# Backward attention: all score gradients transposed by DMA, two units to a transfer

## The chip, the cores and the metric

The kernel runs on one core of a Trainium2 chip. The metric is device time in microseconds (us) of one execution; the number quoted is the median of the runs. A core has TensorE (matrix products, results in PSUM), VectorE, ScalarE and GpSimd (elementwise work), SyncE (SP), which here only starts DMAs, and 16 DMA engines that all queues share. Each engine works through its own instructions in order and waits on semaphores for the others.

## The reference

The reference is one transformer block with conditioned layer norms, and the gradients of its output with respect to nine of its inputs. The sequence has 2048 tokens of 512 features, attention has 32 heads of 16.

```
h = layernorm(x) * (1 + ca) + sa
q, k, v = heads of (h @ wqkv)
p = softmax(q k^T / 4);  x = x + ga * ((p v) @ wo)
h = layernorm(x) * (1 + cb) + sb
x = x + gb * (relu(h @ w1 + b1)^2 @ w2 + b2)
output: x, and the gradients of sum(x * grad_out) for x, wqkv, wo, w1, b1, w2, b2, c, w_mod
```

The change lies in the backward pass of the attention. For each head it needs, with E = p and dP = dO v^T, the matrix dS = E * (dP - rowsum), 2048 x 2048, and from it dK = dS^T q, dV = E^T dO and dQ = dS k.

## The kernel before

Four stages follow each other: projections, forward attention with the feed-forward part and its gradients chunk by chunk, the backward attention loop (1122 to 2409 us in the profile), and a last stage for the remaining gradients.

The backward loop works in units (`units`). A unit is one group of four heads (`hg`), one chunk of 512 keys (`kc`) and one tile of 128 queries (`qc`, `qi`): a piece of 128 queries x 4 heads x 512 keys. There are 8 x 4 x 4 x 4 = 512 units. Four units with the same `hg`, `kc` and `qc` make a block, so there are 128 blocks; unit number `u` belongs to block `u // 4`.

For one unit the work is:

- `score`: four products of 32 x 128 with 32 x 512 into PSUM banks A, B or C (line 1595), one a head. The operands are padded by rows that bring the softmax's maximum and denominator along.
- `expo`: ScalarE takes the exponential of each into the tile `E_u` (line 1601).
- `dp_pair` (a `D` in the order): for two heads at a time two products into `psD_u` (line 1613), and VectorE multiplies them with `E_u` into the tile `dS_u`, 128 x 2048 of bf16, 512 KB (line 1615). Two `D` make a unit's dS.
- `transpose_unit`: after a unit's second `D`, SP starts a transposing DMA from `dS_u` into the unit's quarter of the block's tile `dsT` (line 1628). dQ needs dS with keys on the partitions.
- `k_quad` and `v_quad` (each a `q`): four products each that add the unit's dK and dV to a PSUM bank (lines 1650 and 1659). They read `dS_u` and `E_u` as they are.
- `dq_quad` (in a `d`) and `dq_out` (`Q`): for a whole block, 16 products of `dsT` with the keys (line 1677), and the sum's way out of PSUM by ScalarE (lines 1687 and 1690) and GpSimd (1695).

In every second block (`on_pe`), the fourth unit isn't transposed by DMA. TensorE turns it instead: `pe_turn` (`t1`, `t2`) does eight 128 x 128 transposes into PSUM (line 1640), and ScalarE copies them into `dsT` (`T1`, `T2`, line 1756). So 448 units go over SP's queue and 64 over TensorE.

The order of the work is written out by hand for TensorE, ScalarE, VectorE, SP and GpSimd. Two lists of tokens, `order_n` and `order_t`, each describe one block; block `b` takes `order_t` if block `b - 1` has a TensorE turn. `order_t` has the tokens of the turn and four `f`, which let TensorE do a small product without effect (`keep_warm`, line 1633). In a list, the `s` and `e` belong to block `b`; the `D` run one pair behind them, so a block's last `D` is the first `D` in the next block; the `d1`, `d2` and `Q` belong to block `b - 2`.

How far the stages may run ahead of each other is set by the number of tiles: six of `dS_u`, four of `E_u`, three of `dsT`. A tile is written again when all that read it have finished, so a `dS_u` tile is held until its transfer has landed and its k quad is done. Loads for the next head group are started from ScalarE's queue (`plan_head`), 64 KB each; in the last head group SP itself starts five loads of 512 KB (line 1547).

Of the kernel before, what the change touches and what calls it, by code (L numbers as in the profile page):

```python
# [14 lines left out]
AF = mybir.ActivationFunctionType  # L15
ALU = mybir.AluOpType
AX = mybir.AxisListType
BF = dt.bfloat16
F32 = dt.float32

P = 128
D = 512
# [12 lines left out]
def kernel(  # L35
# [17 lines left out]
    PE = nc.tensor  # L53
    DVE = nc.vector
    ACT = nc.scalar
    POOL = nc.gpsimd
    SP = nc.sync
# [4 lines left out]
    identb = persist.tile([P, P], BF, name="identb")  # L62
# [84 lines left out]
    with ExitStack() as ph:  # L147
# [4 lines left out]
        ework = att.enter_context(tc.tile_pool(name="phCe", bufs=4))  # L152
# [1048 lines left out]
        def head_fill(i):  # L1201
            for key in ("k", "v", "q", "do"):
                POOL.memset(hsets[i][key][:], 1.0 if key in ("k", "v") else 0.0)
# [345 lines left out]
    with ExitStack() as ph:  # L1549
        tpool = ph.enter_context(tc.tile_pool(name="phIt", bufs=3))  # L1550
        ework = ph.enter_context(tc.tile_pool(name="phIe", bufs=4))
        wk = ph.enter_context(tc.tile_pool(name="phIw", bufs=2))
        psd = ph.enter_context(tc.tile_pool(name="psId", bufs=2, space=bass.MemoryType.PSUM))
        psx = ph.enter_context(tc.tile_pool(name="psIx", bufs=1, space=bass.MemoryType.PSUM))
        units = [(hg, kc, qc, qi) for hg in range(HG) for kc in range(QC) for qc in range(QC) for qi in range(4)]
        NU = len(units)
        hst, bst, sst, dqt, cur = {}, {}, {}, {}, {}

        def load_head(hg):
            st = dict(hsets[hg % 2])  # L1560
            st["qz"] = qz[hg % 2]
            st["acc"] = stg.tile([P, n], F32, name="dQacc", tag="dQacc", bufs=1)
            st["dq"] = stg.tile([P, n], BF, name="dQst", tag="dQst", bufs=1)
            st["vk"] = stg.tile([P, n], BF, name="vkb", tag="vkb")
            hst[hg] = st
# [22 lines left out]
        def score(u, hq, bank):  # L1588
            hg, kc, qc, qi = units[u]
            st = hst[hg]  # L1590
            qt = qc * 4 + qi
            r = 32 * hq
            psS = psx.tile([P, 512], F32, name=f"psS_{bank}", tag=banks[bank])
            sst[u, hq] = psS
            PE.matmul(psS[:], st["q"][r:r + 32, qt * P:(qt + 1) * P], st["k"][r:r + 32, kc * 512:kc * 512 + 512],  # L1595
                      start=True, stop=True, tile_position=(r, 0))

        def expo(u, hq):
            if hq == 0:
                bst[u] = [ework.tile([P, 4, 512], BF, name="E_u", tag="E_u"), None]  # L1600
            ACT.activation(bst[u][0][:, hq, :], sst.pop((u, hq))[:], AF.Exp, scale=SCALE)  # L1601

        def dp_pair(u, pair):
            hg, kc, qc, qi = units[u]
            st = hst[hg]
            qt = qc * 4 + qi
            if pair == 0:
                bst[u][1] = ework.tile([P, 4, 512], BF, name="dS_u", tag="dS_u", bufs=6)
            E_u, dS_u = bst[u]
            psD = psd.tile([P, 2, 512], F32, name="psD_u", tag="pd")  # L1610
            for hi in range(2):
                r = 32 * (2 * pair + hi)
                PE.matmul(psD[:, hi, :], st["do"][r:r + 32, qt * P:(qt + 1) * P], st["v"][r:r + 32, kc * 512:kc * 512 + 512],  # L1613
                          start=True, stop=True, tile_position=(r, 0))
            DVE.tensor_tensor(dS_u[:, 2 * pair:2 * pair + 2, :], psD[:], E_u[:, 2 * pair:2 * pair + 2, :], ALU.mult)  # L1615
            if qi == 3 and on_pe(u // 4):
                held["dS"] = dS_u

        def on_pe(b):
            return b % 2 == 1  # L1620

        def transpose_unit(u):
            hg, kc, qc, qi = units[u]
            if qi == 0:
                dqt[u // 4] = tpool.tile([P, 4, 16, P], BF, name="dsT", tag="dsT")
            if qi == 3 and on_pe(u // 4):
                return
            SP.dma_start(out=dqt[u // 4][:, qi], in_=bst[u][1].rearrange("p h k -> p (h k)"), transpose=True)

        held = {}  # L1630

        def keep_warm():
            PE.matmul(cur["vk"][0:DH, :], KS_tok[:, 0, D:QPAD], dOs_tok[:, 0, :], start=False, stop=False,
                      tile_position=(0, 0), skip_group_check=True)

        def pe_turn(b, half):
            pt = psx.tile([P, 8, P], BF, name="ptT", tag="px")
            for i in range(8):
                kt = i % 4
                PE.transpose(pt[:, i, :], held["dS"][:, 2 * half + i // 4, kt * P:(kt + 1) * P], identb[:])  # L1640
            dst = dqt[b][:, 3, 8 * half:8 * half + 8, :]
            held[half] = (dst, pt)

        def k_quad(u):
            hg, kc, qc, qi = units[u]
# [34 lines left out]
        def dq_out(b):  # L1680
# [17 lines left out]
                    r = hg % 2 * 64 + hq * DH  # L1698
                    at(cur["j"] + 6 + hq, load, dQc[hg // 2, r:r + DH, :], st["dq"][32 * hq:32 * hq + DH, :])

        order_t = (
            "s0 s1 q s2 e0 e1 D s3 D e2 s4 e3 t1 e4 q T1 D "
            "s5 s6 e5 f f t2 e6 s7 T2 e7 D s8 e8 D f f s9 e9 q q s10 "
            "s11 e10 D d1 d2 e11 Q q s12 D e12 s13 e13 q s14 D e14 "
            "s15 q q e15 ").split(), "ABCABBABACABABCA"
        order_n = (
            "s0 D s1 q e0 q s2 e1 e2 D s3 s4 q s5 e3 D e4 "
            "e5 s6 q s7 D s8 e6 e7 d1 e8 s9 D d2 e9 q Q s10 "
            "s11 e10 D q s12 e11 e12 s13 e13 D q s14 s15 e14 e15 D q ").split(), "CBACBACBABABCABC"
# [6 lines left out]
        with tc.manual_schedule(engines={PE.engine, ACT.engine, DVE.engine, SP.engine, POOL.engine}):  # L1716
            head_fill(1)
            POOL.memset(qz[1][:], 0.0)
            nD, nq = -1, -4
            idle = psx.tile([P, 512], F32, name="idle", tag="accVK")  # L1720
            for b in range(NU // 4 + 3):
                toks, bank = order_t if on_pe(b - 1) else order_n
                for tok in toks:
                    c, i = tok[0], int(tok[1:] or 0)
                    if c == "s" and b < NU // 4:
                        if i == 0 and units[4 * b][1:] == (0, 2, 0) and units[4 * b][0] + 1 < HG:
                            load_head(units[4 * b][0] + 1)
                        score(4 * b + i // 4, i % 4, bank[i])
                    elif c == "e" and b < NU // 4:
                        expo(4 * b + i // 4, i % 4)  # L1730
                        if b < 2 and i % 2 == 1:
                            if nq > 0:
                                keep_warm()
                            elif nq < 0:
                                PE.matmul(idle[:], ones_bf[:], identb.unsqueeze(1).to_broadcast([P, 4, P]), start=True, stop=True)
                    elif c == "D":
                        if 0 <= nD < 2 * NU:
                            dp_pair(nD // 2, nD % 2)
                            if nD % 2 == 1:
                                transpose_unit(nD // 2)  # L1740
                        nD += 1
                        cur["j"] = nD
                        for j in sorted(j for j in todo if j <= nD):
                            for f, args in todo.pop(j):
                                f(*args)
                    elif c == "q":
                        if 0 <= nq < 2 * NU:
                            (v_quad if nq % 2 else k_quad)(nq // 2)
                        nq += 1
                    elif c == "f" and 0 < nq < 2 * NU:  # L1750
                        keep_warm()
                    elif c == "t" and 0 <= b - 1 < NU // 4:
                        pe_turn(b - 1, i - 1)
                    elif c == "T" and 0 <= b - 1 < NU // 4:
                        dst, pt = held.pop(i - 1)
                        ACT.activation(dst, pt[:], AF.Identity)  # L1756
                    elif c == "d" and 0 <= b - 2 < NU // 4:
                        for kt in (2 * i - 2, 2 * i - 1):
                            dq_quad(b - 2, kt)
                    elif c == "Q" and 0 <= b - 2 < NU // 4:  # L1760
                        dq_out(b - 2)
            assert not todo
        dq_last = hst[HG - 1]["dq"]

    with ExitStack() as ph:
# [15 lines left out]
        order = (("vk", 6), ("vk", 0), ("vk", 1), ("vk", 2), ("vk", 3), ("dq", 0), ("vk", 7), ("dq", 1), ("vk", 4), ("dq", 2), ("vk", 5), ("dq", 3))  # L1781
# [140 lines left out]
        with tc.manual_schedule(engines={PE.engine, ACT.engine, DVE.engine}):  # L1922
            for k, (key, i) in enumerate(order):
                for g in range(2):
                    if (2 * k + g) % 2 == 0:
                        pt = pst.tile([P, 8, P], BF, name="ptq", tag="ptq")
                    else:
                        pt = psd.tile([P, 8, P], BF, name="ptd", tag="pdh1")
                    for ti in range(8):
                        t = 8 * g + ti  # L1930
                        PE.transpose(pt[:, ti, :], xs[key, i][:, t * P:(t + 1) * P], identb[:])
                    if key == "dq":
                        dst = dq_tok[:, 8 * g:8 * g + 8, i * P:(i + 1) * P]
                    else:
                        dst = dvk_tok[:, 8 * g:8 * g + 8, i, :]
# [32 lines left out]
            for b in range(3):  # L1968
                for ic in range(DC):
                    dwqkv(b, ic)  # L1970
                    i = b * DC + ic
# [75 lines left out]
```

## Time and profile before

| | |
|---|---|
| median of 3 runs | 2542.18 us (2538.7 to 2542.64) |
| profiled execution, first to last instruction | 2533.7 us |
| its whole time | not given |
| TensorE products | 2353.2 us (93%), 19005 instructions |
| ScalarE | 2305.1 us (91%), 3577 instructions |
| VectorE | 1808.8 us (71%), 2317 instructions |
| backward loop: dS multiplications on VectorE | 1024 x 1216 ns |
| backward loop: exponentials on ScalarE | 2048 of 650 to 661 ns |
| backward loop: dS transfers on SP | 448, median 2670 ns on SP's queue |
| backward loop: copies after TensorE's turns on ScalarE | 128 x 1128 ns |

The page of a profile gives busy times of the engines, the span in 40 slices, the DMA queues, the chain of work that ended last and the costliest groups. Queries of the trace give single stretches of it: the instructions of one line or tile, the time order of one engine, and sums by stretch. A time on SP's queue is the time that SP itself was occupied with starting a DMA; the transfer lands later. Neighbouring exponentials overlap in ScalarE's pipeline, so their durations add up to more than the time they take.

### The profile page before, as it was taken

How to read it: one execution, taken by the hardware profiler on the slowest of the kernel's cores; microseconds unless marked ns; L12 is line 12 of the kernel's file. 1: busy time of each engine (PE TensorE's matmuls, PEld its weight loads, DVE VectorE, ACT ScalarE, POOL GpSimd, SP SyncE). 2: the span in 40 equal slices, each digit the busy share in tenths (PEclk: the TensorE clock that was granted, in tenths of full speed). 3: DMA queues.
4: the chain of work that ended last, by engine and by line, in shares of the span. 5: the costliest groups of instructions: out<-in, count | busy, mean ns of one | idle time of the engine just before them, and what ended most of it. 6: DMA issues, size and time to landing. Idle time of an engine off the chain costs nothing.

```text
span 2533.7 us, 50560 instructions
## 1 busy us (share of the span) xinstructions
PE 2353.2 (93%) x19005; PEld 777.5 (31%) x19005; DVE 1808.8 (71%) x2317; ACT 2305.1 (91%) x3577; POOL 348.5 (14%) x370
## 2 busy tenths in 40 slices
PE   7898889989988998999999999999999999999999
PEld 3232223223322323533232223232232322332343
DVE  5555153454444455579899999899998998998872
ACT  7999999999999999549999999999999998998952
POOL 2000001211323141110101101011010110100100
PEclk9999999999999999999899999999999999999999
DMA  6477454366649765979999999999999999999972
GB/s 204 126 191 190 140 130 128 90 164 144 94 101 193 129 144 119 276 199 194 189 201 199 198 197 203 197 195 201 206 202 195 202 195 199 202 203 207 200 241 73
DMA packets 1227131, 447.21 MB, mean 177 GB/s; under 512 B 1103096, under 2 KB 1197752, under 8 KB 1226631
## 3 DMA queue, kind: packets, MB, share of 16 engines
q1 hardware_dynamic: 1198966, 409.14, 81.9%
q0 software_dynamic: 10944, 16.78, 4.6%
q10 hardware_dynamic: 16976, 18.07, 2.6%
q8 instruction: 149, 2.44, 0.4%
q14 instruction: 96, 0.78, 0.1%
HBM read 96.75 MB, written 73.95 MB: 67 GB/s over the span
## 4 chain that ended last, share of the span: by engine, by line
PE 41%; ACT 37%; DVE 7%; issue 7%; DMA 5%; SPq 2%; ACTq 0%; POOL 0%; DVEq 0%; POOLq 0%
ACT E_u L1601 23%; ACT ET L562 11%; PE dqacc L1677 5%; PE psST L560 4%; PE psS_A L1595 3%; PE pm L233 3%; DMA dsT<-dS_u 2%; PE accVK L1650 2%; PE oacc L576 2%; PE psS_B L1595 2%; ACT dsT L1756 2%; PE pdh L1871 2%; PE psS_C L1595 2%; SPq L178 2%; PE pm L412 2%
## 5 line engine op out<-in xcount | busy, mean ns | idle before, releaser
L1615 DVE TENSOR_TENSOR dS_u<-psD_u,E_u 128x1024 bf16<-128x1024 f32 x1024 | 1186.1, 1216 | 93.0 <-PE psD_u L1613 27.2
L562 ACT ACTIVATE ET<-psST 128x1024 bf16<-128x1024 f32 x1024 | 942.7, 1240 | 23.4 <-PE psST L560 22.7
L1601 ACT ACTIVATE E_u<-psS_A 128x512 bf16<-128x512 f32 x768 | 507.8, 661 | 14.1 <-DMA out_dram<-xlast 7.2
L1601 ACT ACTIVATE E_u<-psS_B 128x512 bf16<-128x512 f32 x768 | 501.2, 653 | 8.9 <-PE psD_u L1613 2.2
L1613 PE MATMUL psD_u<-iv,ido 32*128 32x512 bf16 x2048 | 412.0, 390 | 5.4 <-DVE dS_u L1615 5.2
L560 PE MATMUL psST<-qt_sb,kt_sb 32*128 32x512 bf16 x2048 | 315.7, 387 | 50.4 <-ACT ET L562 45.5
L1601 ACT ACTIVATE E_u<-psS_C 128x512 bf16<-128x512 f32 x512 | 332.8, 650 | 13.4 <-DMA dsT<-dS_u 9.9
L1595 PE MATMUL psS_A<-ik,iq 32*128 32x512 bf16 x768 | 296.2, 386 | 11.2 <-ACT E_u L1601 1.1
L1595 PE MATMUL psS_B<-ik,iq 32*128 32x512 bf16 x768 | 297.1, 387 | 9.4 <-ACT E_u L1601 1.9
L1595 PEld LDWEIGHTS <-iq 32*128 32x128 bf16 x2048 | 130.0, 91 | 319.1 <-issue 303.4
L1650 PE MATMUL accVK<-dS_u,qz 128*32 128x512 bf16 x2048 | 215.4, 392 | 0.9 <-DVE dS_u L1615 0.6
L576 PE MATMUL oacc<-ET,vaug 128*32 128x512 bf16 x2048 | 207.4, 395 | 3.2 <-DVE ostage L580 3.2
L1659 PE MATMUL accVK<-E_u,dOs_tok 128*16 128x512 bf16 x2048 | 204.6, 388 | 0.0
L1695 POOL TENSOR_TENSOR dQacc<-dQacc,dqtmp 128x512 f32<-128x512 f32 x64 | 81.3, 1270 | 875.5 <-ACT dqtmp L1690 875.5
L1595 PE MATMUL psS_C<-ik,iq 32*128 32x512 bf16 x512 | 195.1, 381 | 4.2
L560 PEld LDWEIGHTS <-kt_sb 32*128 32x128 bf16 x2048 | 85.1, 91 | 339.6 <-issue 319.1
L1677 PE MATMUL dqacc<-dsT,KS_tok 128*32 128x512 bf16 x2048 | 150.1, 392 | 25.2 <-ACT E_u L1601 10.9
L1756 ACT ACTIVATE dsT<-ptT 128x1024 bf16<-128x1024 bf16 x128 | 144.4, 1128 | 10.1 <-PE ptT L1640 9.6
L251 DVE COPY part<-pm 128x512 f32<-128x512 f32 (+2 forms) x103 | 63.4, 616 | 117.6 <-PE pm L233 109.2
L1613 PEld LDWEIGHTS <-ido 32*128 32x128 bf16 x2048 | 105.8, 91 | 105.7 <-issue 99.5
L1650 PEld LDWEIGHTS <-qz 128*32 128x32 bf16 x2048 | 58.9, 94 | 179.2 <-issue 164.9
L576 PEld LDWEIGHTS <-vaug 128*32 128x32 bf16 x2048 | 53.0, 93 | 122.2 <-issue 122.2
(407 smaller groups left out, 2515.4 us busy)
## 6 DMA issues: line engine op xcount, KB each, us to landing
p_st<-part POOLq DMA_DIRECT2D x36, 256.0 KB, 5.2
kt_sb<-qkT_st SPq DMA_DIRECT2D x124, 64.0 KB
wA<-in_B_w_dram SPq DMA_DIRECT2D x28, 256.0 KB
dsT<-dS_u SPq DMA_TRANSPOSE x448
wB<-w1T_st SPq DMA_DIRECT2D x21, 256.0 KB
wA<-w2T_st SPq DMA_DIRECT2D x21, 256.0 KB
wB<-in_B_w_dram SPq DMA_DIRECT2D x21, 256.0 KB
p_st<-part POOLq DMA_DIRECT2D x25, 192.0 KB, 4.2
```

What stands on the lines that cost most here:

```text
L560: PE.matmul(ps[:, hi, :], kt_sb[r:r + 32, kt * P:(kt + 1) * P], qt_sb[r:r + 32, :], start=True, stop=True, tile_position=(r, 0))
L562: ACT.activation(ET[:, 2 * pair:2 * pair + 2, :], ps[:], AF.Exp, scale=SCALE)
L576: PE.matmul(oacc[32 * hq:32 * hq + 32, :], lhsT, ET[:, hq, :], start=(kt == 0), stop=(kt == TT - 1), tile_position=(0, 32 * hq), skip_grou ...
L1595: PE.matmul(psS[:], st["q"][r:r + 32, qt * P:(qt + 1) * P], st["k"][r:r + 32, kc * 512:kc * 512 + 512], start=True, stop=True, tile_positi ...
L1601: ACT.activation(bst[u][0][:, hq, :], sst.pop((u, hq))[:], AF.Exp, scale=SCALE)
L1613: PE.matmul(psD[:, hi, :], st["do"][r:r + 32, qt * P:(qt + 1) * P], st["v"][r:r + 32, kc * 512:kc * 512 + 512], start=True, stop=True, til ...
L1615: DVE.tensor_tensor(dS_u[:, 2 * pair:2 * pair + 2, :], psD[:], E_u[:, 2 * pair:2 * pair + 2, :], ALU.mult)
L1650: PE.matmul(cur["vk"][32 * hq:32 * hq + 32, :], hst[hg]["qz"][:, qt, hq, :], bst[u][1][:, hq, :], start=(qt == 0), stop=False, tile_positi ...
L1659: PE.matmul(acc[32 * hq:32 * hq + DH, :], dOs_tok[:, qt, (hg * 4 + hq) * DH:(hg * 4 + hq + 1) * DH], E_u[:, hq, :], start=False, stop=(qt ...
L1677: PE.matmul(acc[32 * hq:32 * hq + 32, :], KS_tok[:, kc * 4 + kt, h * DH:h * DH + 32], tT[:, :, hq * 4 + kt, :], start=(kt == 0), stop=(kt ...
L1695: POOL.tensor_tensor(dst2, dst, tmp[:], ALU.add)
L1756: ACT.activation(dst, pt[:], AF.Identity)
```

## The change

All 512 units go over SP's queue. Two neighbouring units share one dS tile of 128 x 4096 (1 MB in all), of which there are four, and one transfer carries both, into two quarters of `dsT`. It is started after the second unit's last multiplication. The turns on TensorE, their copies, the `keep_warm` products of `f` and the list `order_t` are gone; every block follows `order_n`, now `order`.

```diff
             if pair == 0:
-                bst[u][1] = ework.tile([P, 4, 512], BF, name="dS_u", tag="dS_u", bufs=6)
+                if qi % 2 == 0:
+                    cur["dS"] = ework.tile([P, 2, 4, 512], BF, name="dS_u", tag="dS_u", bufs=4)
+                bst[u][1] = cur["dS"][:, qi % 2]
...
-            if qi == 3 and on_pe(u // 4):
-                held["dS"] = dS_u
-
-        def on_pe(b):
-            return b % 2 == 1
...
         def transpose_unit(u):
             hg, kc, qc, qi = units[u]
             if qi == 0:
                 dqt[u // 4] = tpool.tile([P, 4, 16, P], BF, name="dsT", tag="dsT")
-            if qi == 3 and on_pe(u // 4):
-                return
-            SP.dma_start(out=dqt[u // 4][:, qi], in_=bst[u][1].rearrange("p h k -> p (h k)"), transpose=True)
-
-        held = {}
+            if qi % 2 == 1:
+                SP.dma_start(out=dqt[u // 4][:, qi - 1:qi + 1].rearrange("p u b q -> p (u b) q"),
+                             in_=cur["dS"].rearrange("p u h k -> p (u h k)"), transpose=True)
...
-        def pe_turn(b, half):
-            pt = psx.tile([P, 8, P], BF, name="ptT", tag="px")
-            for i in range(8):
-                kt = i % 4
-                PE.transpose(pt[:, i, :], held["dS"][:, 2 * half + i // 4, kt * P:(kt + 1) * P], identb[:])
-            dst = dqt[b][:, 3, 8 * half:8 * half + 8, :]
-            held[half] = (dst, pt)
...
-        order_t = (
-            "s0 s1 q s2 e0 e1 D s3 D e2 s4 e3 t1 e4 q T1 D "
-            "s5 s6 e5 f f t2 e6 s7 T2 e7 D s8 e8 D f f s9 e9 q q s10 "
-            "s11 e10 D d1 d2 e11 Q q s12 D e12 s13 e13 q s14 D e14 "
-            "s15 q q e15 ").split(), "ABCABBABACABABCA"
-        order_n = (
+        order = (
             "s0 D s1 q e0 q s2 e1 e2 D s3 s4 q s5 e3 D e4 "
             "e5 s6 q s7 D s8 e6 e7 d1 e8 s9 D d2 e9 q Q s10 "
             "s11 e10 D q s12 e11 e12 s13 e13 D q s14 s15 e14 e15 D q ").split(), "CBACBACBABABCABC"
...
-                toks, bank = order_t if on_pe(b - 1) else order_n
+                toks, bank = order
...
-                    elif c == "f" and 0 < nq < 2 * NU:
-                        keep_warm()
-                    elif c == "t" and 0 <= b - 1 < NU // 4:
-                        pe_turn(b - 1, i - 1)
-                    elif c == "T" and 0 <= b - 1 < NU // 4:
-                        dst, pt = held.pop(i - 1)
-                        ACT.activation(dst, pt[:], AF.Identity)
```

## The prediction

> **What bounds the kernel now.** I read the page first, then the stretch that the change touches: the backward loop, from 1126 us (first dS transfer) to 2408 us. From the page:
>
> ```profile
> span 2533.7 us, 50560 instructions
> PE 2353.2 (93%) x19005; PEld 777.5 (31%) x19005; DVE 1808.8 (71%) x2317; ACT 2305.1 (91%) x3577; POOL 348.5 (14%) x370
> DMA  6477454366649765979999999999999999999972
> ...
> q1 hardware_dynamic: 1198966, 409.14, 81.9%
> ```
>
> Three things are nearly full at once: TensorE, ScalarE, and from the 18th slice on the DMA engines. Which of them sets the loop's pace? First the engines, in four consecutive blocks (a block is four units and 16 exponentials), blocks with a TensorE turn and without one in turn; the columns are the stretch, its length, busy time with instruction counts per engine, granted clock, DMA share, GB/s:
>
> ```profile
> 1802.99:1813.77 10.78, 10.43 (x107) 3.74 (x110) 10.00 (x9) 10.78 (x21) 0.00 (x0) 1.00 1.16 182
> 1813.77:1822.29 8.52, 8.25 (x78) 2.09 (x78) 8.52 (x9) 8.48 (x18) 0.00 (x0) 1.00 1.09 230
> 1822.29:1832.89 10.60, 10.22 (x107) 3.74 (x110) 9.82 (x9) 10.51 (x20) 1.81 (x2) 1.00 1.17 201
> 1832.89:1841.41 8.52, 8.25 (x78) 2.16 (x78) 8.52 (x9) 8.48 (x18) 3.47 (x2) 1.00 1.18 204
> ```
>
> A block with a turn takes 10.7 us, one without 8.52 us, and in both ScalarE is full. 64 x (10.7 + 8.52) = 1230 us; the loop takes 1276 us. So today the engines set the pace for all but some 46 us.
>
> Then SP's queue. The rows are start, length from the first start to the last end, and count, from the time order of SP in five stretches: one transfer alone, another alone, four of 128 KB in a row in the phase before, then the transfers begun by 1715 us, and the loop from 1491 us on:
>
> ```profile
> 1126.15 1.93 SPq L1628 DMA_TRANSPOSE dsT<-dS_u  x1
> ...
> 1139.45 1.92 SPq L1628 DMA_TRANSPOSE dsT<-dS_u  x1
> ...
> 1109.25 5.16 SPq L178 DMA_TRANSPOSE dOT<-dOs_c  x4
> ...
> 1126.15 589.59 SPq L1628 DMA_TRANSPOSE dsT<-dS_u  x204
> ...
> 1490.87 772.54 SPq L1628 DMA_TRANSPOSE dsT<-dS_u  x273
> ```
>
> Alone, SP is done with a 512 KB transfer in 1.93 us. Later, 273 of them take 772.54 us, 2.83 us each. Is that SP waiting for VectorE? The table of SP's waits says so (962.6 us), but the counts speak against it. By 1715 us VectorE had begun this many dS multiplications:
>
> ```profile
> 1120.00:1715.00 595.00, 546.51 (x472) 0.96 1.15 195
> ```
>
> 472 are 236 units; less the 29 that TensorE turns, 207 are for SP. It had begun 204, so about three units lay ready behind the one in work. That table names the last semaphore event inside an instruction's duration, which here is of a later unit. So the transfers are backlogged: 2.83 us is what the queue can do under load, not what it is asked for. At times the backlog uses up the buffers, and the chain shows engines waiting for it:
>
> ```profile
> 1606.35 6.56 DMA dsT<-dS_u
> ...
> 1622.62 6.85 DMA dsT<-dS_u
> ```
>
> Seven transfers of 2.83 us are 19.8 us against 19.2 us of engine time for two blocks. The loop is bound by both, nearly equal.
>
> What sets the 2.83 us? The rate of the first 20 us of the loop, in 40 slices of 0.5 us:
>
> ```profile
> GB/s 0 0 50 218 208 219 209 145 0 0 0 113 246 167 5 9 171 290 283 290 289 251 14 140 211 215 218 205 60 144 211 211 219 185 224 211 206 227 213 187
> ```
>
> A lone transfer runs at 208 to 219 GB/s, mean 213: 524,288 B take 2.46 us. After a stop (slices "5 9") it runs at 283 to 290 GB/s (1.81 us) until that is made good. I read this as descriptors arriving at 213 GB/s, and a store of them drained faster after a stop. The stops go with 16 KB loads on the instruction queue; of the loop alone:
>
> ```profile
> q10 hardware_dynamic: 12080, 14.40, 4.3%
> q8 instruction: 91, 1.49, 0.4%
> q14 instruction: 52, 0.43, 0.1%
> ```
>
> 0.4% of 16 engines over 1276 us is 82 us, 0.9 us a load. Over the whole loop (447 steps from 1126.15 to 2401.7 us) a unit costs 2.85 us: 2.46 of data at the lone rate, 0.39 of starts and stops.
>
> **The change, part by part.**
>
> *64 more units on the queue.* 64 x 2.85 = +182 us, on the path, since SP never catches up.
>
> *Joining two units.* 512 starts become 256. No row shows what a start costs behind a running transfer. One end: nothing, as the next is made ready while the last one's data still flow (in the packet records the median gap between one transfer's last packet and the next one's first is 3 ns). Other end: all of the 0.39 us, 256 x 0.39 = -100 us. I take the mean of that gap, 0.12 us, the nearest row: -31 us. Could a longer transfer cost more than two short ones? 128 KB and 512 KB, 1.29 and 2.83 us apart, show growth below proportion, so I exclude it.
>
> *Stops.* 102 us of instruction loads (82 + 20) lie in the 448 units and don't grow with them: 64 x 102/448 = -15 us. The loop has 30,000 instructions; some 2,700 go (1024 transposes with their weight loads, 256 warming matmuls with theirs, 128 copies), 9% of 102 us: -9 us. End values 0 and -24, and 0 if the starts are given all of the 0.39 us. I take -24 us.
>
> *TensorE, ScalarE and PSUM.* Every block becomes the 8.52 us kind: 128 x 8.52 = 1091 us, 139 us less engine work (128 copies of 1.13 us on ScalarE are most of it). Worth nothing, because four units need about 10.9 us of the queue; if that cover were gone, the loop would be 185 us shorter. Instead about 2.4 us of waiting appears in each block.
>
> *Buffers and waits.* Six single dS tiles become four double ones. The multiplication that opens a pair now waits for the transfer issued six units before it, where it was five, and the first dqacc quads of a block for its second pair, issued at the start of the block after it: 1.3 blocks, 14 us of a stretched block. Behind the waiting multiplication stand k quads and all of VectorE; behind the quads, scores and so ScalarE. A pair takes 5.5 us plus the queue; SP keeps at least one pair ready through such a wait, so these waits are the form that the queue's pace takes and no addition to it. In between nothing new stands on SP; the loads on ScalarE's queue keep their places. I price the part at 0.
>
> *End.* The last transfer is twice as long: +2.46 us, rounded to 3.
>
> Sum: 182 - 31 - 24 + 3 = +130 us. The profiled execution spans 2533.7 us (its whole time isn't given); with 130, 2664. The median of the runs is 8.5 us above that span: 2672. Ends: 182 - 100 + 3 = +85 (2627) and +185 (2727).
>
> A rule in favour of joining is weighed against the 2.83 us row (185 GB/s): the Trainium skill, DMA: Bandwidth & Descriptors, "Latency and other measured facts", gives a transposing DMA 261 GB/s with a strided middle dimension. By the page a pair takes 4.0 us as an estimate, the queue would be no bound any more, and the sum would be -185 us instead of +130.
>
> A rule against the change stands beside the same row: the Trainium skill, VectorE: DVE Perf Modes, "Rules for kernel authors", turns 128x128 blocks on TensorE where PSUM will do, with 390 ns for it and 1309 ns for the DMA crossbar in its table of paths. A unit has 16 such blocks, so 64 units would cost about 940 us more by the page (an estimate); the row, 0.18 us a block, has the direction but not the size.
>
> **The rivals.**
>
> *A start is dear, and joining pays (faster).* Put a line through 128 KB in 1.29 us and 512 KB in 2.83: 0.78 us a start and 0.51 us per 128 KB, so 4.9 us a pair; 256 x 4.9 = 1254, 22 us under today: 2520. If the faster rate (290 GB/s, 3.6 us a pair) held throughout, the engines would bound and 2357 were possible. It decides below 4.98 us a pair. For it: the 290 GB/s slices. Against: the small transfers are bound by issue (1.29 us apart for 0.62 us of data at 213 GB/s), and there the two don't add, and a lone 512 KB runs at 213 GB/s after its start is paid.
>
> *Joining saves nothing*, by cost or because the transfer is split again: +185, 2727. For it: the 3 ns median gap.
>
> *The queue runs empty.* If it waited once a block for a pair's second unit, two multiplications of some 1.13 us, 128 x 2.3 = 290 us come on top: about 2960. And waits over 3 us have so far been followed by half clock (0.93 granted between 1200 and 1300 us), which hits the engines where they have slack. Against it: by the order of the tokens a block's pairs are complete at 1.9 and, with the wait, at 8.6 us of it, and under load SP gets to them at 9.6 and 15.0 us, over 6 us later.
>
> **How the numbers follow.** Queue-bound with joining worth little to something: 0.72; nothing saved: 0.10; queue empty: 0.06; starts dear: 0.12, of which 0.03 within 0.2% (about what a measurement of this kernel can tell from no change, 5 us). Slower 0.88, same 0.03, faster 0.09. The range takes in the ends, 2627 and 2727, and some margin on each side, down into the dear starts: 2595 to 2740.
>
> **What would show it.** 256 transfers of dS on SP, 5.2 to 5.7 us apart with no idle between; all blocks near 10.9 us, with a wait of 2 to 2.5 us for dsT or a dS tile; the chain's DMA share from 5% to 15% or more; ScalarE busy about 145 us less. Pairs under 4.98 us apart, or SP idle between them, would make the forecast wrong.

## The result and the profile after

The changed kernel takes 2661.36 us (median of 4 runs, 2661.05 to 2666.04), the kernel before 2540.45 us beside it: a ratio of 1.0487, 95% interval 1.0464 to 1.0509, or 121 us more. The forecast was 2672 us, in a range of 2595 to 2740.

The page of the changed kernel, the lines that answer to those shown of before, and the clock:

```profile
span 2659.6 us, 47020 instructions
PE 2321.6 (87%) x17635; PEld 689.8 (26%) x17724; DVE 1821.7 (68%) x2317; ACT 2220.3 (83%) x3449; POOL 347.8 (13%) x370
...
PEclk9998999999999999978888887888887888988889
DMA  7476562468577759799999999999999999999982
...
q1 hardware_dynamic: 1323894, 442.67, 84.5%
...
PE 46%; ACT 24%; DMA 14%; DVE 7%; issue 6%; SPq 1%; ACTq 1%; another core or an unknown queue 0%; DVEq 0%; POOL 0%
```

Two lines of the page of before, for comparison:

```profile
PEclk9999999999999999999899999999999999999999
...
PE 41%; ACT 37%; DVE 7%; issue 7%; DMA 5%; SPq 2%; ACTq 0%; POOL 0%; DVEq 0%; POOLq 0%
```

Every compute engine is busy for a smaller share of the span (VectorE, in us, for as long as before), the DMA engines are full from the 18th slice on, and the chain's DMA share has risen from 5% to 14%. New is the clock row: the granted clock of TensorE, 0.9 or more in nearly all slices before, is between 0.7 and 0.9 in nearly all slices of the loop.

The transfers in the time order of SP (start, length, count), and the same by tile (shortest, median and longest time on SP's queue in ns, first and last start):

```profile
1133.19 1238.58 SPq L1624 DMA_TRANSPOSE dsT<-dS_u  x227
```

```profile
L1624 SPq DMA_TRANSPOSE dsT<-dS_u x256: 4801/5235/6797, 1133.2 to 2526.4; - x128
```

227 transfers of 1 MB take 1238.58 us without a longer pause, 5.46 us each. From the first to the last start the loop takes 1393.2 us, against 1275.6 before: +117.6 us. The first transfer starts 7.0 us later (1133.2 against 1126.2 us), and what comes after the last start is 1.2 us longer. That is all of the 125.9 us between the two spans.

How do the engines get through a block now? Two blocks of the changed kernel (stretch, length, busy time with counts of TensorE, its weight loads, VectorE, ScalarE and GpSimd, granted clock, DMA share, GB/s):

```profile
1773.83:1783.01 9.18, 8.12 (x84) 2.22 (x88) 9.08 (x9) 8.65 (x18) 1.27 (x1) 1.00 1.20 220
1792.78:1804.83 12.05, 11.30 (x87) 2.29 (x88) 9.57 (x9) 9.11 (x17) 1.27 (x1) 0.59 1.18 211
```

One block takes 9.18 us at full clock, the other 12.05 us at a granted clock of 0.59, and the loop is a mixture of such blocks, 10.88 us on average ((2519.8 - 1126.7)/128, by the first exponential and the end of the last). So there are two suspects for the same 121 us: the queue that the forecast named, and a slow TensorE. They had to be told apart.

### The profile page after: what moved, and what is told of

It reads as the page before. It is cut to its first block, busy times and chain, and to the rows that moved or that the text cites. A ratio compares the mean times of both kernels' runs of the same rounds, so it can differ in the third digit from the quotient of the medians.

```text
span 2659.6 us, 47020 instructions
## 1 busy us (share of the span) xinstructions
PE 2321.6 (87%) x17635; PEld 689.8 (26%) x17724; DVE 1821.7 (68%) x2317; ACT 2220.3 (83%) x3449; POOL 347.8 (13%) x370
## 4 chain that ended last, share of the span: by engine, by line
PE 46%; ACT 24%; DMA 14%; DVE 7%; issue 6%; SPq 1%; ACTq 1%; another core or an unknown queue 0%; DVEq 0%; POOL 0%
ACT E_u L1601 12%; DMA dsT<-dS_u 12%; ACT ET L562 10%; PE dqacc L1664 6%; PE psS_B L1595 4%; PE psST L560 4%; PE psS_A L1595 4%; PE psS_C L1595 3%; PE accVK L1637 3%; PE accVK L1646 3%; PE pm L233 2%; PE oacc L576 2%; PE pm L412 2%; PE pdh L1846 2%; PE pwq L1880 2%
## 5 line engine op out<-in xcount | busy, mean ns | idle before, releaser
L1601 ACT ACTIVATE E_u<-psS_B 128x512 bf16<-128x512 f32 x768 | 470.0, 612 | 118.8 <-PE psD_u L1615 92.3
L1615 PE MATMUL psD_u<-iv,ido 32*128 32x512 bf16 x2048 | 455.8, 442 | 0.4 <-DVE dS_u L1617 0.4
L1601 ACT ACTIVATE E_u<-psS_C 128x512 bf16<-128x512 f32 x640 | 393.8, 615 | 74.5 <-PE psS_B L1595 61.4
L1601 ACT ACTIVATE E_u<-psS_A 128x512 bf16<-128x512 f32 x640 | 395.8, 618 | 34.8 <-PE psD_u L1615 19.2
L1595 PE MATMUL psS_B<-ik,iq 32*128 32x512 bf16 x768 | 338.3, 440 | 26.8 <-ACT E_u L1601 15.5
L1595 PE MATMUL psS_C<-ik,iq 32*128 32x512 bf16 x640 | 269.7, 421 | 101.6 <-ACT E_u L1601 100.2
L1664 PE MATMUL dqacc<-dsT,KS_tok 128*32 128x512 bf16 x2048 | 201.5, 479 | 78.6 <-DMA dsT<-dS_u 51.7
L1637 PE MATMUL accVK<-dS_u,qz 128*32 128x512 bf16 x2048 | 237.9, 453 | 1.2 <-DVE dS_u L1617 0.9
L1664 PEld LDWEIGHTS <-KS_tok 128*32 128x32 bf16 x2048 | 40.1, 99 | 197.5 <-issue 167.3
L1646 PEld LDWEIGHTS <-dOs_tok 128*16 128x16 bf16 x2048 | 49.8, 87 | 149.4 <-issue 149.4
```

Source lines behind the costliest of these rows:

```text
L1637: PE.matmul(cur["vk"][32 * hq:32 * hq + 32, :], hst[hg]["qz"][:, qt, hq, :], bst[u][1][:, hq, :], start=(qt == 0), stop=False, tile_positi ...
L1646: PE.matmul(acc[32 * hq:32 * hq + DH, :], dOs_tok[:, qt, (hg * 4 + hq) * DH:(hg * 4 + hq + 1) * DH], E_u[:, hq, :], start=False, stop=(qt ...
L1664: PE.matmul(acc[32 * hq:32 * hq + 32, :], KS_tok[:, kc * 4 + kt, h * DH:h * DH + 32], tT[:, :, hq * 4 + kt, :], start=(kt == 0), stop=(kt ...
```

## The experiments

Times are medians. The kernel before took 2543.4, 2541.3 and 2540.6 us beside the three groups of runs; differences to it are taken within a group.

**One transfer a unit.** What does a start cost behind a running transfer? All 512 units still go by DMA, but not joined.

```diff
-            if qi % 2 == 1:
-                SP.dma_start(out=dqt[u // 4][:, qi - 1:qi + 1].rearrange("p u b q -> p (u b) q"),
-                             in_=cur["dS"].rearrange("p u h k -> p (u h k)"), transpose=True)
+            SP.dma_start(out=dqt[u // 4][:, qi], in_=bst[u][1].rearrange("p h k -> p (h k)"), transpose=True)
```

> The changed kernel with one transfer of 512 KB a unit in place of one of 1 MB a pair; tiles, order and work are the same. It has 256 starts more. If a start behind a running transfer costs 0.12 us (the forecast), the time is 2661 + 31 = 2692 us. If it costs nothing, it stays at 2661. If it costs all of the 0.39 us that a unit took above its data in the kernel before, it is 2761.

Measured: 2693.7 us (2691.9 to 2698.4), 32 us above the changed kernel, 0.126 us a start. "Nothing" and 0.39 us are out, and the forecast's 0.12 is close. It isn't quite the price of a start, though. The transfers of this kernel:

```profile
L1623 SPq DMA_TRANSPOSE dsT<-dS_u x512: 1682/2622/4645, 1129.3 to 2562.4; - x171
```

From the first to the last start this loop takes 1433.1 us, 39.9 us more than the changed kernel's, 0.16 us a start. But its first transfer begins 3.9 us earlier, and what comes after its last start is 3.7 us shorter.

**Two transfers a unit.** The same with 256 KB.

```diff
+            for hp in range(2):
+                SP.dma_start(out=dqt[u // 4][:, qi, 8 * hp:8 * hp + 8], in_=bst[u][1][:, 2 * hp:2 * hp + 2].rearrange("p h k -> p (h k)"), transpose=True)
```

> The changed kernel with two transfers of 256 KB a unit, one for each pair of heads, both issued after the unit's second multiplication: 1024 starts, 768 more than the changed kernel. At 0.12 us a start the time is 2661 + 92 = 2753 us; at nothing it stays at 2661 (two starts of 1.3 us still fit into a unit's 2.73 us); at 0.39 us a start it is about 2960. If the time is in proportion to the starts, the rise over the changed kernel is three times that of the run with 512 KB.

Measured: 2795.2 us (2787.0 to 2797.3), 134 us above the changed kernel, 0.174 us a start. That is more than 0.12, and four times the rise of the run before, not three times; the step from 512 to 256 KB alone costs 0.198 us a start. SP's time order from 1300 to 2300 us, of the changed kernel with 1 MB:

```profile
1299.29 1003.87 SPq L1624 DMA_TRANSPOSE dsT<-dS_u  x185
```

Of the kernel with 512 KB:

```profile
1298.15 1005.43 SPq L1623 DMA_TRANSPOSE dsT<-dS_u  x360
```

Of the kernel with 256 KB:

```profile
1298.91 1003.14 SPq L1624 DMA_TRANSPOSE dsT<-dS_u  x672
```

A unit takes 1003.87/370 = 2.71 us with half a start, 1005.43/360 = 2.79 us with one and 1003.14/336 = 2.99 us with two. From two starts to one it saves 0.19 us, from one to half 0.08. At that rate a unit without any start would still take some 2.63 us (an estimate), so joining more than two units could save at most about 40 us over the 512 units. It wasn't run.

**Joined, but with the turns.** The kernel before with one part of the change: two units in a transfer wherever both go by DMA, in four double tiles.

```diff
-                bst[u][1] = ework.tile([P, 4, 512], BF, name="dS_u", tag="dS_u", bufs=6)
+                if qi % 2 == 0:
+                    cur["dS"] = ework.tile([P, 2, 4, 512], BF, name="dS_u", tag="dS_u", bufs=4)
+                bst[u][1] = cur["dS"][:, qi % 2]
...
-            if qi == 3 and on_pe(u // 4):
-                return
-            SP.dma_start(out=dqt[u // 4][:, qi], in_=bst[u][1].rearrange("p h k -> p (h k)"), transpose=True)
+            if qi == 2 and on_pe(u // 4):
+                SP.dma_start(out=dqt[u // 4][:, qi], in_=bst[u][1].rearrange("p h k -> p (h k)"), transpose=True)
+            elif qi % 2 == 1 and not (qi == 3 and on_pe(u // 4)):
+                SP.dma_start(out=dqt[u // 4][:, qi - 1:qi + 1].rearrange("p u b q -> p (u b) q"),
+                             in_=cur["dS"].rearrange("p u h k -> p (u h k)"), transpose=True)
```

> The kernel before, with its turns on TensorE, but units 0 and 1 of every block and units 2 and 3 of a block without a turn in one transfer; unit 2 of a block with a turn goes alone. 448 units in 256 transfers. Theory: the queue and the engines bind equally in the kernel before, 7 units take 3 x 5.46 + 2.85 = 19.2 us instead of 19.9 against 19.2 us of engine work, so a good half of the 46 us of waiting goes: 2505 to 2520 us. Rival: the 46 us come from bursts of other transfers, which joining doesn't change, and the double tiles hold buffers longer: 2540 or more.

Measured: 2519.1 us (2513.7 to 2533.7), a ratio of 0.9916 to the kernel before (0.9888 to 0.9944). The longest pieces of the chain that are waits for dsT, in this kernel (they began at 1747, 2118, 2176 and 2309 us; the kernel before had eleven of over 4 us):

```profile
1747.21 8.31 DMA dsT<-dS_u
2118.65 8.26 DMA dsT<-dS_u
2176.63 7.90 DMA dsT<-dS_u
2309.26 6.25 DMA dsT<-dS_u
```

So joining, with the double tiles that it needs, is a gain of 24 us, and this kernel beats both others. (The four double tiles hold eight units where there was room for six; what that part gives wasn't measured apart.) The loss is in sending the 64 units over the queue.

**Half the data.** What would the loop take if the queue were no bound? Only the first unit of a pair is transposed, and the dQ products read its result twice, so that TensorE's work stays; the second unit's part of dQ is left out.

```diff
-                dqt[u // 4] = tpool.tile([P, 4, 16, P], BF, name="dsT", tag="dsT")
+                dqt[u // 4] = tpool.tile([P, 2, 16, P], BF, name="dsT", tag="dsT")
...
-                SP.dma_start(out=dqt[u // 4][:, qi - 1:qi + 1].rearrange("p u b q -> p (u b) q"),
-                             in_=cur["dS"].rearrange("p u h k -> p (u h k)"), transpose=True)
+                SP.dma_start(out=dqt[u // 4][:, qi // 2], in_=cur["dS"][:, 0].rearrange("p h k -> p (h k)"), transpose=True)
...
-                PE.matmul(acc[32 * hq:32 * hq + 32, :], KS_tok[:, kc * 4 + kt, h * DH:h * DH + 32], tT[:, :, hq * 4 + kt, :],
+                PE.matmul(acc[32 * hq:32 * hq + 32, :], KS_tok[:, kc * 4 + kt, h * DH:h * DH + 32], tT[:, :, hq * 4 + kt, :].unsqueeze(1).to_broadcast([P, 2, 2, P]),
```

> The changed kernel, but only the first unit of each pair is transposed (512 KB a pair), and the dQ products read its result twice, so that TensorE has the same work; the second unit's part of dQ is left out. The queue needs 256 x 2.85 = 730 us and binds no more, so this is the loop's time by its engines alone. By the forecast's 8.52 us a block the loop takes 1091 us and the kernel 2661 - (1393 - 1091) = 2360 us. Rival: 8.52 us was measured between two long blocks, in which VectorE caught up; 1024 multiplications 1.13 us apart are 1157 us and the shortest blocks of the changed kernel take 9.14 us, so the loop takes 1170 us and the kernel 2440.

Measured: 2557.7 us (2534.7 to 2571.8), no faster than the kernel before, rather 0.5% slower (ratio 1.0049, 1.0026 to 1.0072). Neither theory had that. Two of its blocks, from the profile of its fastest run:

```profile
1744.37:1753.55 9.18, 8.12 (x84) 2.22 (x88) 9.18 (x9) 8.65 (x18) 1.27 (x1) 1.00 0.62 117
1835.33:1847.39 12.06, 11.31 (x86) 2.29 (x88) 9.69 (x9) 9.11 (x18) 1.88 (x2) 0.59 0.49 94
```

They are the two kinds of block of the changed kernel, here with the DMA share near half of what it was. The block at full clock has VectorE busy all the time, as the second theory said. The other kind has TensorE busy for 11.3 of 12.06 us at half clock for most of it (half clock was granted 41 times in the kernel, 32 of them in the loop). So the new order without turns loses its clock with the queue far from full, and its engines alone need about as long as the whole old loop.

**Half the data, with added products.** Is it the clock? Four small products without effect (`keep_warm`) in each block.

```diff
-            "e5 s6 q s7 D s8 e6 e7 d1 e8 s9 D d2 e9 q Q s10 "
-            "s11 e10 D q s12 e11 e12 s13 e13 D q s14 s15 e14 e15 D q ").split(), "CBACBACBABABCABC"
+            "e5 f s6 q s7 D s8 e6 e7 d1 e8 f s9 D d2 e9 q Q s10 "
+            "s11 e10 D q s12 e11 f e12 s13 e13 f D q s14 s15 e14 e15 D q ").split(), "CBACBACBABABCABC"
...
+                    elif c == "f" and 0 < nq < 2 * NU:
+                        keep_warm()
```

> The half-data kernel (second unit of a pair not transposed, its part of dQ left out) with four small products without effect added to every block, where TensorE would wait. Without them its blocks took 9.15 us at full clock and about 12.06 us where half clock was granted, 41 times, and the kernel 2558 us. Theory: the half clock comes from too little work on TensorE, not from the waits for DMA; with the added products the clock stays near 1.0, blocks take 9.15 us, the loop 1171 us and the kernel about 2440. Rival: the added work (4 x 0.2 us a block) only adds to TensorE's time, or the clock falls for another reason: 2540 to 2600.

Measured: 2578.3 us (2566.4 to 2581.7). The clock did hold (0.982 over the span), but most blocks took 9.94 us, all alike: at these places the products lengthen a block. Between 1500 and 1900 us VectorE was busy for 91% and TensorE for 89%, so neither was full; which wait grew was not followed up. Half of the theory, and no answer on the time.

**Half the data, products in the gap.** Two products a block, at the place where TensorE waits anyway. In the half-data kernel this is the wait of the block's first score for bank C (time order of TensorE, the idle time before it in brackets):

```profile
1753.14 0.37 PE L1595 MATMUL psS_C<-ik,iq 32*128 32x512 bf16 x1 [0.75 <-ACT E_u L1601]
```

```diff
-            "s11 e10 D q s12 e11 e12 s13 e13 D q s14 s15 e14 e15 D q ").split(), "CBACBACBABABCABC"
+            "s11 e10 D q s12 e11 e12 s13 e13 D q s14 s15 e14 e15 D q f f ").split(), "CBACBACBABABCABC"
...
+                    elif c == "f" and 0 < nq < 2 * NU:
+                        keep_warm()
```

> The half-data kernel (second unit of a pair not transposed, its part of dQ left out) with only two small products a block, both in the one place where TensorE waits 0.75 us in a block of 9.15 us: ahead of the next block's first score, which waits for ScalarE to empty bank C. The kernel with four at other places kept the clock at 0.98, but its blocks took 9.94 us throughout. Theory: the clock is what lengthened the half-data kernel's blocks; two products of some 0.25 us in the gap cost nothing and hold it: blocks of 9.15 us, 2440 us. Rival: two are too few and the clock still falls, or the block lengthens by their time: 2480 to 2560.

Measured: 2473.2 us (2469.6 to 2478.8), 84 us less than without them, for more work. Three stretches of 100 us, then one of the half-data kernel without the products for comparison in the second fence:

```profile
1500.00:1600.00 100.00, 92.02 (x880) 24.51 (x876) 97.48 (x86) 93.24 (x184) 13.60 (x11) 0.98 0.70 123
1600.00:1700.00 100.00, 91.95 (x850) 24.04 (x847) 95.76 (x84) 91.53 (x179) 11.60 (x8) 0.95 0.72 129
1700.00:1800.00 100.00, 91.92 (x885) 24.86 (x885) 98.55 (x87) 94.28 (x187) 7.98 (x7) 1.00 0.73 128
```

```profile
1900.00:2000.00 100.00, 88.75 (x777) 22.15 (x777) 91.45 (x80) 86.83 (x170) 10.34 (x7) 0.86 0.65 117
```

The clock is what lengthened the half-data kernel's blocks. The theory's 2440 us were not reached: some half clock is left, and every fourth block is about 0.5 us longer.

**The changed kernel with added products.** If the slow clock were a cause of the 121 us, restoring it should give part of them back.

```diff
-            "e5 s6 q s7 D s8 e6 e7 d1 e8 s9 D d2 e9 q Q s10 "
-            "s11 e10 D q s12 e11 e12 s13 e13 D q s14 s15 e14 e15 D q ").split(), "CBACBACBABABCABC"
+            "e5 f s6 q s7 D s8 e6 e7 d1 e8 f s9 D d2 e9 q Q s10 "
+            "s11 e10 D q s12 e11 f e12 s13 e13 f D q s14 s15 e14 e15 D q ").split(), "CBACBACBABABCABC"
...
+                    elif c == "f" and 0 < nq < 2 * NU:
+                        keep_warm()
```

> The changed kernel with the same four small products a block. The clock granted in its loop is 0.80 to 0.87. Forecast's theory: the transfer queue sets the pace and the half clock falls into time that the engines wait anyway: 2661, within 5 us. Rival: the slow clock is a cause of the loss in its own right: 2600 or less, as far towards the half-data kernel as the clock counts.

Measured: 2666.9 us (2661.4 to 2672.7). Three stretches of it, then the same of the changed kernel in the second fence:

```profile
1800.00:1900.00 100.00, 89.16 (x811) 25.22 (x810) 87.95 (x77) 85.33 (x164) 8.34 (x7) 0.97 1.19 206
1900.00:2000.00 100.00, 85.31 (x776) 23.87 (x775) 85.84 (x75) 81.90 (x158) 13.37 (x10) 0.97 1.19 202
2000.00:2100.00 100.00, 84.90 (x752) 23.52 (x745) 83.33 (x73) 80.57 (x156) 9.07 (x6) 0.95 1.18 209
```

```profile
1800.00:1900.00 100.00, 87.90 (x740) 20.83 (x732) 85.69 (x74) 81.98 (x158) 6.78 (x6) 0.80 1.18 206
1900.00:2000.00 100.00, 87.25 (x760) 21.33 (x759) 89.29 (x77) 84.90 (x165) 14.98 (x11) 0.85 1.18 207
2000.00:2100.00 100.00, 86.54 (x728) 20.53 (x724) 85.00 (x74) 82.26 (x159) 9.08 (x6) 0.81 1.22 206
```

The clock is back at 0.95 to 0.97 (0.80 to 0.85 without the products), the DMA share and rate are hardly changed, and the time is no better (5.5 us above the changed kernel's, with the ranges overlapping). The added products don't hide a gain here: by the half-data run with the same products the engines alone would get through most blocks in 9.94 us, and the loop still takes 10.91 us a block. The slow clock fills time that the engines would spend waiting for the queue; it adds nothing while the queue binds.

**More instructions.** Does a stop for an instruction load cost the stream? First on GpSimd.

```diff
+            spare = stg.tile([1, 4], F32, name="spare", tag="spare", bufs=1)
             for b in range(NU // 4 + 3):
+                if 2 <= b < NU // 4:
+                    for _ in range(60):
+                        POOL.memset(spare[:], 0.0)
```

> The changed kernel with 60 tiny memsets a block added on GpSimd, which is idle there: 126 x 60 = 7560 instructions, some 30 more instruction loads of 16 KB. Theory of the forecast: each such load stops the transposing stream for about 1 us and the stops are paid: 2661 + 27 = 2688. Rival: the stream makes the stops good out of its store of descriptors: 2661 to 2668.

Measured: 2667.6 us (2659.6 to 2674.1), no clear difference. But it isn't a test: the added loads of this kernel's loop were of the other, smaller kind.

```profile
q8 instruction: 81, 1.33, 0.4%
q14 instruction: 106, 0.87, 0.2%
```

The changed kernel has 81 and 47 there. 59 more small loads cost no more than the runs differ among themselves.

**More instructions on TensorE.**

```diff
-            "s11 e10 D q s12 e11 e12 s13 e13 D q s14 s15 e14 e15 D q ").split(), "CBACBACBABABCABC"
+            "s11 e10 D q s12 e11 e12 s13 e13 D q s14 s15 e14 e15 D q f f ").split(), "CBACBACBABABCABC"
...
+                    elif c == "f" and 0 < nq < 2 * NU:
+                        for _ in range(16):
+                            PE.matmul(cur["vk"][0:DH, 0:8], KS_tok[:, 0, D:QPAD], dOs_tok[:, 0, 0:8], start=False, stop=False,
+                                      tile_position=(0, 0), skip_group_check=True)
```

> The changed kernel with 32 tiny products of 8 columns a block on TensorE, at the same place, where the changed kernel's TensorE has time to spare. With their weight loads they are some 8000 instructions more and, at 330 instructions a 16 KB load as in the loop so far, 24 loads more (the memsets on GpSimd made none of these). Theory of the forecast: every such load costs the transposing stream about 1 us: 2661 + 24 = 2685. Rival: the stream makes the stops good from its store: 2661 to 2668. More than 2690 would mean that TensorE itself became the bound.

Measured: 2681.4 us (2675.1 to 2686.6), 20 us more than the changed kernel. The loop's loads:

```profile
q8 instruction: 113, 1.85, 0.5%
q14 instruction: 47, 0.39, 0.1%
```

The run has 32 loads of 16 KB more (113 against 81) and takes 20 us more: 0.63 us each, if the loads are all of it. The time is lost on the queue: 183 transfers take 1006.32 us on SP from 1300 to 2300 us, 5.50 us each against 5.43, and over the loop SP waits for a late multiplication for 13.5 us in all, against 10.1 us in the changed kernel. So at most some 3 us came by TensorE's own longer work; that the added products slow the transfers in another way isn't excluded.

**Three tiles.** One double dS tile less (`bufs=4` to `bufs=3`).

> The changed kernel with three double dS tiles in place of four. Theory: SP has at least one pair ready even so, the waits only move: 2661 to 2668. Rival: the number of tiles limits, and the queue runs empty once a block for two multiplications (2.3 us): 2661 + 290 = 2950; every microsecond a block would show as 128 us.

Measured: 2659.9 us (2658.8 to 2667.0): no difference. Buffers don't set the pace.

## Why the prediction was right, and where it wasn't

*The queue binds.* Shown from three sides: SP's transfers follow each other without pause, starts that are added or taken away move the time by themselves, and neither a better clock nor a tile less moves it. Over the whole loop SP waited about 10 us for a multiplication to end (19 us in the kernel before).

*64 more units, +182, less 24 for the stops, gives +158 before joining.* The run with one transfer a unit is this step alone: 2693.7 against 2543.4 us, +150, and between the two profiles the loop, from first to last start, is 157.5 us longer (1433.1 against 1275.6). The step holds as a sum, but not for the reason given. A unit's step fell from 2.85 to 2.80 us, about 25 us over 511 steps, as large as the credit. With 0.63 us a load, though, the stops give only some 13 (91 loads are 57 us; a seventh of that is 8, and 9% of it 5); another 4 us are SP's shorter waits (14.5 us against 18.7). What gave the rest is open.

*Joining, -31 us, and end, +3.* Together -28; measured -32, and here two errors offset each other. The 0.12 us was the mean gap between two transfers, not a price of a start, and it was too low: at 0.16 us a start joining saves 39.9 us from first to last start. The ends take back 7.6 us, not 3: the first transfer also waits for the pair's second unit, 2.4 us here (1130.73 to 1133.13 us), which the sum left out. Against the kernel before, the first transfer starts 7.0 us later; 4.2 of these were there before the loop, where the kernels are alike (the first exponential starts at 1126.72 instead of 1122.50 us).

*From the span to the median, +8.5 us.* The runs whose span is given take 1.7 to 2.2 us more than it, the profiled one of the changed kernel 1.8. So the profiled execution of the kernel before, with its 2533.7 us, was faster than any of the four runs beside the changed kernel, and most of the 8.5 was that. It is the larger part of the 11 us by which the forecast is high; from span to span the forecast was +130, measured +125.9 us.

*TensorE, ScalarE and PSUM: "139 us less engine work", and "if that cover were gone, the loop would be 185 us shorter".* This step failed. With the queue relieved, the kernel took 2557.7 us: nothing was there to be gained. Two things were missed. The 8.52 us block was measured between two long blocks, in which VectorE did a part of its work; eight multiplications 1.13 us apart are 9.04 us, and no block of the kernels without turns ran under 9.14. And with the turns and the `f` products TensorE's clock had stayed up (half clock for 75 us of the loop); without them it falls more often, and a block at half clock takes 12.05 us. With the clock mostly held, the half-data kernel took 2473 us. The step was priced at nothing because the queue covers it, so the sum didn't suffer; had the queue run at 290 GB/s throughout, as one rival allowed, that rival's 2357 us would have been wrong by about 200.

*Buffers and waits, priced at 0.* Held, with the caution that the waits hardly look like waits. The forecast was "all blocks near 10.9 us, with a wait of 2 to 2.5 us for dsT or a dS tile"; the average is 10.88, but single blocks take 9.2 or 12 us, and much of the queue's time shows as TensorE running at half clock.

*ScalarE busy 145 us less.* It was 85 less (2305.1 to 2220.3). The copies' own durations were subtracted, but they overlap with their neighbours': in the trace of before, ScalarE's busy time without the copies is 2211.6 us, only 93.5 less.

*Half clock after waits over 3 us.* That was too narrow a reading. In the loop of before, three of the sixteen periods of half clock follow an idle time of TensorE of over 3 us. The two between 1200 and 1300 us, which made the 0.93, don't: the longest idle time there is 0.37 us.

*The rates weighed in the forecast.* A transposing DMA at 261 GB/s (the Trainium skill, DMA: Bandwidth & Descriptors, "Latency and other measured facts") isn't reached here: 1 MB every 5.43 us (1003.87/185) is 193 GB/s beside the other traffic. The 1309 ns for a 128x128 block over the crossbar (the Trainium skill, VectorE: DVE Perf Modes, "The three transpose paths") is not what a block costs in a long transfer: 5.43 us for 32 blocks is 0.17 us. The rule of that page's "Rules for kernel authors", to transpose on TensorE where PSUM will do, was right here for the 64 units: sending them over the queue cost 150 us.

## What to carry to other kernels

Before moving work onto a queue, count what is ready for it against what it has begun: a queue with work lying ready has no room, however long its waits in a table. Joining transfers and moving work to them are two changes; here the first, with its double tiles, is worth 24 us and the second costs 150. And don't blame a low clock for a loss before it has been restored by itself. Here TensorE's clock fell while the queue set the pace, its slow work stood where the waiting would have been, and restoring it gained nothing; with the queue relieved, restoring it gained 84 us.

## What the runs showed of the hardware

TensorE's clock can fall to half without a long idle time of TensorE. In the half-data kernel's loop no idle time of TensorE between 1200 and 2390 us is longer than 1.56 us, the regular one is 0.75 us in a block of 9.18 us, and half clock was granted for 294 us of the loop in 32 periods. Two products of 0.25 us in that gap brought it to 68 us in 13 periods. The Trainium skill, TensorE: Matmul & The Clock Gate, "Part 1: The HAM clock gate (the "warmup" mystery)", puts the fall behind an idle window of about 3.4 us; the shortest periods here are of that length (3.41 us), but the idle time ahead of them isn't. The same part also tells of a kernel in which frequent short idle times made the clock swing, and that is nearer to this case. What brings the clock down here stays open: from 1200 us on, the 3.41 us ahead of a fall held 0.5 to 1.0 us of idle time in 27 of 28 cases, but there are stretches of that length with 0.9 us that no fall followed.
